# Reassociating the second product of an attention + MLP + soft-MoE kernel

## The chip, the cores and the metric

One NeuronCore of a Trainium2 chip runs the whole program. The metric is device time in microseconds. TensorE (PE) multiplies and writes to PSUM; VectorE (DVE), ScalarE (ACT) and GpSimd (POOL) work element by element; SyncE (SP) issues the DMAs. PEld in the profile is TensorE's load of a stationary operand, which overlaps its matmuls.

## The reference

```python
def reference(q, k, v, moe_w_in, moe_w_out, moe2_phi, moe2_w1, moe2_w2):
    # 4 batches x 8 heads x 576 tokens x 64; heads 0-3 look back 32 tokens,
    # heads 4-7 at tokens of the same residue mod 32
    a = attention(q, k, v)                       # softmax(mask(q k^T / 8)) v
    x = a.transpose(0, 2, 1, 3).reshape(2304, 512)
    r = np.maximum(x @ w_in, 0)                  # w_in 512 x 2048
    g = r * r
    x2 = g @ w_out                               # w_out 2048 x 512
    logits = x2 @ phi                            # phi 512 x 32
    d = softmax(logits, axis=0)                  # over the 2304 tokens
    slot_input = d.T @ x2                        # 32 x 512
    # 8 experts, 4 slots each: relu(slot_input w1[e]) w2[e], 512 -> 1024 -> 512
    c = softmax(logits, axis=1)                  # over the 32 slots
    return c @ slot_out
```

## The kernel before, in words

The 2304 tokens are cut into six blocks of T = 384. The work goes in three stretches.

The head is written out by hand in `HEAD` (L29), a list of small steps for all engines: scores (`S`), centring (`C`), exponential and normalising (`E`), transposing (`T`) and values (`V`, `U`) of the attention units. A unit is two heads of a batch; units 0 to 3 are batch 0. It also loads the weights (`l`), and converts them two tiles at a time: `split1` to `split4` (`W`, `X`, `Y`) take 64-bit words apart (ACT, then DVE) and make a high and a low float32r part (ACT, then DVE). `w_in` and `w_out` are both converted so, 32 tiles, 16 pairs; raw tiles sit in slots that converted tiles take later. Idle PE time is filled with `keep_warm` matmuls (L579).

The middle runs over g, which counts 6 blocks x 16 slices f of d_ff. PE and SP follow the program order there; the order on DVE, ACT and POOL is made by a scheduler that goes by priority, which is program order, with `square` put ahead. `gemm1(g)` (L401) has `w_in` stationary and the block's x moving, 12 matmuls of 384 columns (three high/low products of four kc); its result is h transposed, 128 of d_ff by 384 tokens. `square` and `square_low` make g's high and low part (L408 to L417). `gemm2(g-1)` (L423, L426) has g stationary and a `w_out` tile moving, 9 matmuls of 512 columns, summed over f in three banks, one for 128 tokens each. At the end of each block these sums are copied out as x2 (L439), and `Dispatch` follows, spread over the next block at `MOE_AT`: `tr` transposes x2 (L450), `logits` multiplies it by phi (L469, 32-wide weights at three column positions side by side), `soft`, `back` (L515) and `slots` (L521) hold a running maximum, running sums and a running slot input `acc`, and `comb0`, `comb1` make the softmax over slots. The attention of batches 1 to 3 runs between (`BATCHES`).

The expert weights are 64 tiles of 512 KB: `e0` to `e31` of w1, `e32` to `e63` of w2. `load_e`, `load_e_ring` and `load_e_slot` put them where room has come free: five tiles when the attention's memory goes, then the rings of x, then, all through the last block, two weight slots per g.

The tail takes the softmax of the last block to its end, makes `siT` (L773), multiplies by w1 (`gemm_a`, L812, `eh` in the trace), refills tiles (`refill`), then by w2 (`gemm_b`, L836), and forms the output from the slot outputs (`output`, L859 to L864). `gemm_b(1, 0)` is the first to need the last w2 tile; the two outputs of `slot_out`, the second half of `gemm_b` and 18 output DMAs stand behind it.

Of the kernel before, what the change touches and what calls it, by code (L numbers as in the profile page):

```python
# [28 lines left out]
HEAD = 'w0 w0 w0 w0 w0 w0 k0 q0 q2 l3 l2 q1 S0 S2 S0 w0 w0 w0 W1 l0 S2 S2 w0 S0 W1 l1 v2 w0 S0 S0 C0 w0 l4 C2 W1 E0 W1 w0 E0 W1 W1 S1 X1 X1 E2 W0 w0 Y1 E0 E2 E0 q3 w0 W0 l5 S1 E2 T0 w0 S1 T0 E2 S3 l10 w0 W0 S1 W0 T2 S1 w0 C1 W0 v0 T0 T0 l18 T0 w0 X0 T2 X0 T0 E1 T0 w0 Y1 l7 T0 S3 W0 w0 W0 E1 Y0 T2 T2 w0 v3 V0 T2 E1 E1 V0 T2 S3 w0 T2 T2 T2 l6 V0 W0 w0 C3 E3 U0 E3 T1 v1 T1 w0 l11 U0 W0 D1 W3 T1 W3 E3 w0 V2 D1 T1 E3 W2 l9 Y0 w0 D1 W3 T1 g4 V2 l15 V2 D1 U2 T3 U2 W2 V1 T3 W2 g0 W3 V1 W2 U1 g2 W3 l19 T3 T3 T3 V1 q6 g6 l20 T3 X3 Y3 T3 T3 T3 U1 g1 X3 X2 g5 V3 V3 W3 W2 Y3 U3 l16 V3 X2 Y2 l14 l8 W5 U3 S6 Y2 S6 g3 W5 W5 S6 W5 W2 R0 g7 q4 R1 g10 R1 R1 R0 W5 R0 l12 C6 E6 E6 W5 W4 g8 g14 g9 X5 l17 L1 H0 g11 E6 L0 W4 H1 W4 v6 Y5 X5 Y5 O1 W4 E6 T6 l26 W4 R2 R2 g18 R2 W7 g17 W7 T6 l13 W7 g16 g13 g12 W4 X4 Y4 O0 X4 l27 g15 l28 R3 p0 T6 g19 T6 Y4 W7 R3 R3 S4 W6 g20 l21 X7 W7 g22 S4 L3 W6 L2 H2 W7 S4 W6 R4 H3 q5 R4 R4 X7 g21 Y7 W6 S5 H4 O2 X6 W6 Y7 g23 W9 S4 L4 Y6 X6 C4 W9 E4 O3 g26 R5 E4 W9 R5 q7 Y6 W6 E4 W9 O4 E4 R5 g24 g30 W8 l22 L5 W8 T4 W9 g25 g27 H5 X9 R6 R6 l23 X9 W8 Y9 W9 T4 Y9 W11 T4 W8 g32 g28 T4 T4 g34 X8 W8 g29 R6 g35 T4 H6 W8 Y8 W11 O5 X8 W11 W10 L6 g31 R7 R7 T4 g33 R8 S7 Y8 T4 W11 O6 W10 R8 S5 W11 S5 H7 g36 R7 V6 L7 S5 R8 X11 S7 W11 W10 v4 O7 V6 X11 L8 S7 C5 g42 E5 W10 V6 E5 W10 Y11 Y11 E5 g37 O8 U6 X10 W13 l24 X10 Y10 W13 g38 g40 g39 E5 H8 Y10 V4 T5 W13 W13 U6 l25 R9 g41 W13 T5 g44 W12 g43 V4 T5 T5 C7 T5 W13 g46 U4 W10 l29 W12 R10 v5 W12 W13 g45 R9 g47 g49 g50 R10 T5 R9 R10 g48 L10 H9 H10 L9 g51 W12 W13 R11 E7 X13 T5 O10 E7 Y13 R11 l30 X12 T5 V5 R11 W12 X12 V5 O9 R12 Y12 g53 Y12 L11 g55 R12 X13 E7 U5 R12 Y13 L12 H11 g56 W14 W13 E7 T7 W14 g54 W14 W12 T7 W14 T7 g52 O11 O12 g58 T7 R13 R13 T7 T7 l31 g57 X14 R13 W14 v7 L13 X14 g59 H12 T7 Y14 T7 T7 Y14 T7 W14 W15 g62 W15 R14 R14 T7 T7 W15 H13 T7 T7 R14 T7 W15 T7 O13 L14 W15 T7 V7 X15 g60 X15 Y15 V7 H14 V7 Y15 O14 g61 U7 W15 U7 g63 R15 R15 R15 L15'.split()  # L29
BATCHES = [(1, 16, (0, 1), (4, 8), (0, 1, 2, 3, 5), (2, 1)), (2, 32, (0, 2, 1, 3), (0, 3, 6, 9), (0, 1, 2, 3, 5), (2, 1)), (3, 48, (0, 2, 1, 3), (0, 3, 6, 9), (0, 1, 2, 3, 5), (2, 1))]  # L30
MOE_AT = (1, 2, 3, 5, 7, 9, 10, 11)
ATT_END = 64
PRIO = 400
LOW = 'DDDPDDDDPPDPDPPP'
SUB = 'DDDDDDDDDDDDDDDD'
WARM = 6
# [24 lines left out]
def body(tc, qd, kd, vl, vs, win, wout, phi, w1, w2, cst, out):  # L61
# [3 lines left out]
    with ExitStack() as base, ExitStack() as order:  # L65
# [9 lines left out]
        bp = pool(base, "bp", side="right")  # L75
# [16 lines left out]
        elT = cp.tile([128, 2, 128], F32, name="elT")
# [5 lines left out]
        tf = cp.tile([128, NS], F32, name="tf")  # L98
# [3 lines left out]
        bt = bp.tile([128, 6, 512], F32, name="bt")  # L102
# [13 lines left out]
        def slot(n, shape, dt, name):  # L116
# [3 lines left out]
        bflat = bt.rearrange("p a b -> p (a b)")  # L120
# [217 lines left out]

        NW = 2 * NF
        w_in, w_out = [None] * NF, [None] * NF
        raws, ys = {}, {}

        def load_w(n):
            if n < 26:  # L350
                raws[n] = slot(n + (8 if n < 22 else 4), [128, 512, 2], U32, f"raw{n}")
            else:
# [584 lines left out]
```

## Time and profile before

| | |
|---|---|
| median of 3 runs | 558.02 us (557.0 to 558.48) |
| span of the profiled execution | 557.1 us |
| busy: PE / PEld | 535.7 us (96%) / 451.6 us (81%) |
| busy: DVE / ACT / POOL | 252.1 / 248.2 / 44.2 us |
| moved by DMA | 72.88 MB, mean 131 GB/s |
| chain that ended last, by engine | PE 80%, DMA 7%, DVE 6%, ACT 3% |
| chain, by line | L401 33%, L426 23%, L423 11% |

The profile is that of one execution, so sums are made against its span. A busy PE is not a PE at its peak, because matmuls overlap and each one's recorded duration holds its neighbours; what a matmul adds is read from the chain of waits, where pieces follow one another. A float32 matmul is recorded as two instructions, a float32r matmul and a transpose as one. "L401" is a line of the kernel before.

### The profile page before, as it was taken

What the parts mean: (1) busy time and instruction counts of PE and PEld (TensorE: products, weight loads), DVE (VectorE), ACT (ScalarE), POOL (GpSimd) and SP (SyncE); (2) the same over time, 40 slices, a digit from 0 to 9 for tenths busy, and PEclk for the clock granted to TensorE, in tenths of its full rate; (3) what the DMA queues carried; (4) which work ended last, traced back from release to release, by engine and by line L of the source; (5) the groups of instructions that cost most, each with busy time, mean ns of one, the idle gap of its engine ahead of it and who ended that gap; (6) DMA issues with size and microseconds to landing.
All of it is one profiled execution on the core that took longest, in us unless ns stands there. A gap on an engine that the chain in (4) does not pass through costs nothing.

```text
span 557.1 us, 10035 instructions
## 1 busy us (share of the span) xinstructions
PE 535.7 (96%) x4098; PEld 451.6 (81%) x4098; DVE 252.1 (45%) x593; ACT 248.2 (45%) x545; POOL 44.2 (8%) x56
## 2 busy tenths in 40 slices
PE   9689999999999999999999999999999999999993
PEld 7467888889888888888888888898899988985552
DVE  5988999841544156473265482311311113114213
ACT  1379787774442344433454343443333533334213
POOL 2101113110110010020010200000000000001000
PEclk9699999999999999999999999999999999999998
DMA  8987634210102011202011201610002557678958
GB/s 234 358 311 246 253 102 165 99 35 0 44 1 67 24 44 44 82 25 81 25 44 51 74 25 39 259 44 1 0 2 98 186 220 251 227 267 333 388 199 288
DMA packets 27118, 72.88 MB, mean 131 GB/s; under 512 B 3008, under 2 KB 8640, under 8 KB 27072
## 3 DMA queue, kind: packets, MB, share of 16 engines
q1 hardware_dynamic: 27072, 72.24, 37.2%
q8 instruction: 32, 0.52, 0.4%
q14 instruction: 14, 0.11, 0.1%
HBM read 67.51 MB, written 4.72 MB: 130 GB/s over the span
## 4 chain that ended last, share of the span: by engine, by line
PE 80%; DMA 7%; DVE 6%; ACT 3%; issue 1%; SPq 1%; POOL 1%; DVEq 0%; ACTq 0%; POOLq 0%
PE h L401 33%; PE acc_ps L426 23%; PE acc_ps L423 11%; DMA k<-kd 3%; DMA e<-w 2%; DMA ring<-w 2%; PE oa L313 2%; PE ob L313 2%; PE x2t L450 1%; DVE w L388 1%; PE lg L469 1%; PE qa L193 1%; PE acc_ps L836 1%; PE warm L579 1%; DVE y L374 1%
## 5 line engine op out<-in xcount | busy, mean ns | idle before, releaser
L401 PE MATMUL h<-xr,w 128*128 128x384 f32 x1152 | 220.5, 338 | 1.5 <-DVE xr L332 1.0
L401 PEld LDWEIGHTS h<-xr,w 128*128 128x128 f32 x1152 | 204.3, 188 | 11.2 <-DVE xr L332 1.2
L426 PE MATMUL acc_ps<-w,gh 128*128 128x512 f32 x576 | 153.1, 401 | 0.2 <-ACT gh L411 0.2
L408 ACT ACTIVATE r<-h 128x384 f32<-128x384 f32 x96 | 47.1, 490 | 196.3 <-PE h L401 194.9
L426 PEld LDWEIGHTS acc_ps<-w,gh 128*128 128x128 f32 x576 | 103.9, 188 | 24.7 <-ACT gh L411 2.9
L417 DVE TENSOR_TENSOR gl<-r,gh 128x384 fp32r<-128x384 f32 x89 | 49.9, 561 | 163.5 <-ACT r L413 159.5
L423 PE MATMUL acc_ps<-w,gl 128*128 128x512 f32 x288 | 82.2, 393 | 0.2 <-DVE gl L417 0.2
L423 PEld LDWEIGHTS acc_ps<-w,gl 128*128 128x128 f32 x288 | 53.8, 188 | 12.0 <-DVE gl L417 0.3
L411 ACT ACTIVATE gh<-r 128x384 fp32r<-128x384 f32 x96 | 50.3, 525 | 2.8
L413 ACT ACTIVATE r<-r 128x384 f32<-128x384 f32 x96 | 50.2, 525 | 2.1
L247 DVE STREAM_TRANSPOSE ptl<-sl 32x320 f32<-32x320 f32 (+2 forms) x72 | 31.3, 435 | 8.7 <-POOL sl L234 7.6
L365 ACT ACTIVATE y<-raw 128x512 f32<-128x512 f32 x26 | 17.0, 670 | 14.6 <-DMA raw<-win 13.1
L388 DVE TENSOR_TENSOR w<-y,w 128x512 fp32r<-128x512 f32 x30 | 22.2, 748 | 2.6 <-ACT w L381 2.4
L381 ACT CAST w<-y 128x512 fp32r<-128x512 f32 x30 | 18.4, 618 | 10.5 <-DVE y L374 10.4
L219 POOL TENSOR_TENSOR sl<-sl,tiny 128x640 f32<-128x640 f32 (+2 forms) x9 | 10.8, 1202 | 138.8 <-DVE tiny L216 138.8
L579 PE MATMUL warm<-el 128*128 128x256 f32 x66 | 20.3, 461 | 1.1 <-POOL el L572 1.1
L579 PEld LDWEIGHTS warm<-el 128*128 128x128 f32 x66 | 14.8, 236 | 4.1 <-POOL el L572 1.1
L374 DVE SCALAR_TENSOR_TENSOR y<-raw,y 128x512 uint32<-128x512 uint32 x26 | 17.4, 681 | 0.2
L202 DVE SCALAR_TENSOR_TENSOR sl<-qa,c 128x128 f32<-128x128 f32 (+3 forms) x18 | 6.4, 376 | 21.5 <-PE qa L193 16.5
L792 POOL MEMSET bt<- 128x512 f32 x4 | 2.0, 525 | 174.9 <-PE lg L469 172.8
L247 DVE STREAM_TRANSPOSE pts<-sw 32x512 f32<-32x512 f32 x20 | 14.1, 703 | 3.7 <-POOL sw L234 3.4
L836 PE MATMUL acc_ps<-e,bt 128*32 128x192 f32 (+1 forms) x184 | 14.9, 380 | 0.5 <-DMA e<-w 0.5
(187 smaller groups left out, 439.0 us busy)
## 6 DMA issues: line engine op xcount, KB each, us to landing
e<-w SPq DMA_DIRECT2D x49, 512.0 KB, 4.8
ring<-w SPq DMA_DIRECT2D x15, 512.0 KB, 8.2
raw<-win SPq DMA_DIRECT2D x14, 512.0 KB, 7.6
raw<-wout SPq DMA_DIRECT2D x12, 512.0 KB, 6.7
q<-qd SPq DMA_DIRECT2D x15, 288.0 KB, 3.1
k<-kd SPq DMA_DIRECT2D x30, 144.0 KB, 3.7
v<-vs SPq DMA_DIRECT2D x7, 512.0 KB, 3.2
out<-ob SPq DMA_DIRECT2D x9, 320.0 KB, 3.9
```

The lines of the kernel that those rows point to most:

```text
L247: DVE.transpose(out=dst, in_=src)
L313: PE.matmul(o[bank][64 * h:64 * h + 64, col:col + w1_ - w0], u.v[0:k, t, 64 * h:64 * h + 64], rhs, start=start, stop=stop, skip_group_chec ...
L374: DVE.scalar_tensor_tensor(out=yb, in0=raws[2 * m + z][:, :, 0], scalar=29, in1=yb, op0=ALU.logical_shift_right, op1=ALU.bitwise_or)
L388: (POOL if SUB[m] == "P" else DVE).tensor_tensor(out=w[:, 1], in0=ys[m][:, z], in1=w[:, 0].bitcast(F32), op=ALU.subtract)
L401: PE.matmul(hs[g][0][:, 0:T], w_in[f][:, a, 128 * kc:128 * kc + 128], xr[i % 3][:, x, kc, :], start=hs[g][1] == 0, stop=hs[g][1] == 11)
L408: ACT.activation(r, h[:, 0:T], AF.Relu)
L411: ACT.activation(gh[g], r, AF.Square)
L413: ACT.activation(r, r, AF.Square)
L417: (POOL if LOW[g:g + 1] == "P" else DVE).tensor_tensor(out=gl[g], in0=rs.pop(g), in1=gh[g].bitcast(F32), op=ALU.subtract)
L423: PE.matmul(a, gl[g][:, 128 * j:128 * j + 128], w[:, 0], start=False, stop=f == NF - 1)
L426: PE.matmul(a, gh[g][:, 128 * j:128 * j + 128], w[:, z], start=f == 0 and z == 0, stop=False)
L579: PE.matmul(warm[:, 0:256], a, b, start=True, stop=True)
```

## The change

The second product is never formed. Since logits = x2 phi = g (w_out phi), the kernel makes `pt` = w_out phi once (`turn_w` transposes w_out tiles, `phi_w` multiplies them by phi), and the logits from g transposed and `pt`. Since d^T x2 = (d^T g) w_out, the slot sums are taken of g, 32 x 2048 held as 128 x 512 in `acc`, and `w_out` is applied once, in the tail.

The first product is turned round: x is stationary (128 tokens) and `w_in` moves, 512 wide. There are 72 steps s (6 blocks x 4 chunks ch of 512 x 3 token groups j) with 12 matmuls each. `square` is one ReLU; `tr` transposes the four 128 x 128 parts of its result, ACT squares them on the way out of PSUM, and POOL (from block 4 on DVE) squares the untransposed copy in place. `w_in` is still converted to a high and low part, `w_out` to float32 alone. The w_out tiles' raw buffers are three (`rawp`). The head is shorter and ordered by hand for PE and SP only; what was in `HEAD` for batch 1, and the conversion of `w_out`, moves to numbered places (`PLACES`, four per step). `load_e` calls move with the buffers. The expert products and the output keep their form.

```diff
-W_ORDER = [(0, 0), (0, 1), (0, 2), (1, 0)] + [w for f in range(3, NF) for w in ((0, f), (1, f - 2))] + [(1, NF - 2), (1, NF - 1)]
+W_ORDER = [(c, kc) for c in range(4) for kc in (0, 2, 1, 3)]
+AT = [2, 8, 14, 22, 46, 60, 74, 86, 98, 110, 122, 134, 146, 158]
+OFF = [0, 4, 8, 12, 23]
+PLACES = [(0, "l16"), (0, "l17"), (0, "l18")]
+for n, p in enumerate(AT):
+    PLACES += [(AT[n - 1] + 2 if n else 0, f"q{n}"), (AT[n - 1] + OFF[4] if n else 0, f"v{n}")]
+    PLACES += [(p + o, k + str(n)) for k, o in zip("SCETV", OFF)]
+for m in range(8):
+    PLACES += [(8 + 4 * m, f"c{m + 8}")] + [(10 + 4 * m, f"l{n}") for n in range(19 + 2 * m, min(21 + 2 * m, 32))]
+PLACES += [(18 + 2 * f, f"z{f}") for f in range(16)] + [(20 + 2 * f, f"p{f}") for f in range(16)]
+TR0 = [30, 31, 32, 35, 36, 37, 40, 41, 42, 45, 46, 49]
...
+            if m < 8:
+                if m < 2:
+                    ys["t", m] = slot(16 + m, [128, 2, 512], F32, f"y{m}")
+                ys[m] = ys["t", m % 2]
+            else:
+                ys[m] = slot(8 + m, [128, 2, 512], F32, f"wo{m}")
...
+        def gemm1(s, kcs=range(4)):
...
+                for x, a in ((0, 0), (0, 1), (1, 0)):
+                    PE.matmul(hs[s][0], xr[b % 3][:, x, kc, 128 * j:128 * j + 128], w_in[ch, kc][:, a],
...
+        def tr(s):
...
+            o = ps("t", f"t{s}")
+            for y in range(4):
+                PE.matmul(o[:, 128 * y:128 * y + 128], gs[b, ch][:, j, 128 * y:128 * y + 128], ident, start=True, stop=True,
+                          is_transpose=True)
+            ACT.activation(gts[b, ch][:, :, 128 * j:128 * j + 128], o.rearrange("p (y t) -> p y t", y=4), AF.Square)
+            g = gs[b, ch][:, j]
+            (POOL if b < 4 else DVE).tensor_tensor(out=g, in0=g, in1=g, op=ALU.mult)
+        def logits(b, ch):
...
+            for y in range(4):
+                PE.matmul(lgs[b][32 * y:32 * y + 32, 0:T], pt[:, 4 * ch + y, :], g[:, y, :], start=ch == 0, stop=ch == 3,
+                          skip_group_check=True)
+        def turn_w(f):
+            o = ps("at", f"wt{f}")
...
+            ACT.copy(wts[f], o)
+        def phi_w(f):
...
+            for kc in range(4):
+                PE.matmul(pps[0][:, 32 * y:32 * y + 32], wts[f][:, 128 * kc:128 * kc + 128], ph[:, kc, :],
+                          start=kc == 0, stop=kc == 3, skip_group_check=True)
...
+            def total(self):
+                self.o = ps("mo", f"lr{self.b}")
+                PE.matmul(self.o[:, 0:T], tident, lsb, start=True, stop=True)
...
+            def turn(self):
+                o = self.o2 = ps("mo", f"lt{self.b}")
                 for j in range(3):
+                    lt = lsb[:, 128 * j:128 * j + 128]
+                    PE.matmul(o[:, 96 + 32 * j:128 + 32 * j], lt, tident[:, 0:NS], start=True, stop=True)
+                    PE.matmul(o[:, 32 * j:32 * j + 32], lt, tident[:, 0:NS], start=True, stop=False)
+                    PE.matmul(o[:, 32 * j:32 * j + 32], quarter, dg, start=False, stop=True)
+                ACT.activation(ex_, o[:, 0:96], AF.Exp)
...
+            def slots(self):
+                o = ps("mo", f"sa{self.b}")
+                for j in range(3):
+                    for ch in range(4):
+                        PE.matmul(o[32 * ch:32 * ch + 32, :], ex_[:, 32 * j:32 * j + 32], gs[self.b, ch][:, j, :],
+                                  start=j == 0, stop=j == 2, skip_group_check=True)
+                DVE.scalar_tensor_tensor(out=acc, in0=acc, scalar=al, in1=o, op0=ALU.mult, op1=ALU.add)
...
+            for kc in range(4):
+                if s > 1 or kc == 3:
+                    gemm1(s, (0, 2, 1, 3)[kc:kc + 1])
+                if kc == 3:
+                    with tc.high_priority(offset=PRIO):
+                        square(s)
+                for fn, args in bg.get(4 * s + kc, ()):
+                    fn(*args)
+            if s > 60 and s % 3 == 2:
+                for n in range(4 * ((s - 60) // 3), 4 * ((s - 60) // 3) + 4):
+                    load_e_slot(n)
...
+        o = ps("lg", "si")
+        for y in range(4):
+            for ch in range(4):
+                PE.matmul(o[32 * ch:32 * ch + 32, :], gT[:, y, 32 * ch:32 * ch + 32], w_out[4 * ch + y],
+                          start=y == 0, stop=y == 3, skip_group_check=True)
...
+        for n in range(16, 24):
+            load_e_slot(n)
```

The head in the changed order has, for PE: 24 warm matmuls, scores of units 0, 2 and 1 with warm matmuls between, values of unit 0, scores of unit 3, values of 2, the first product's kc 0 and 2 of steps 0 and 1, values of 1, kc 1, values of 3. Converts 0 and 1 stand in it; converts 2 to 7 follow it, ahead of step 0's last kc.

## Rows read from the trace of the kernel before

**Rows 1.** The page's forty slices: granted TensorE clock in tenths of full speed.

```profile
PEclk9699999999999999999999999999999999999998
```

**Rows 2.** Windows: stretch, its length, busy us (instructions) of each engine, clock, DMA.

```profile
9.80:49.05 39.25, 30.66 (x430) 24.42 (x421) 34.34 (x74) 22.01 (x54) 2.99 (x3) 0.87 0.87 297
49.05:497.40 448.35, 447.13 (x3080) 391.31 (x3081) 195.94 (x449) 207.54 (x448) 35.73 (x35) 1.00 0.27 91
497.40:557.10 59.70, 49.18 (x533) 28.74 (x532) 17.22 (x65) 17.34 (x43) 1.98 (x4) 0.95 0.82 305
```

**Rows 3.** Chain of waits, middle and start of tail: start, us, what, instructions.

```profile
371.33 2.11 PE h L401 x12
373.43 0.44 PE x2t L450 x4
373.87 1.39 PE acc_ps L426 x6
...
382.24 1.00 PE lg L469 x24
383.25 1.60 PE acc_ps L426 x6
...
400.40 0.99 PE sa L521 x6
401.39 1.59 PE acc_ps L426 x6
...
509.69 3.56 PE eh L812 x32
```

**Rows 4.** Groups by line of PE, 49.05 to 497.4: count, busy us, mean ns.

```profile
L401 PE MATMUL h<-xr,w 128*128 128x384 f32 x1133 | 216.0, 337 | 1.0 <-DVE xr L332 1.0
L426 PE MATMUL acc_ps<-w,gh 128*128 128x512 f32 x565 | 150.1, 401 | 0.2 <-ACT gh L411 0.2
L423 PE MATMUL acc_ps<-w,gl 128*128 128x512 f32 x282 | 80.1, 393 | 0.2 <-DVE gl L417 0.2
```

**Rows 5.** Timeline of PE, 10 to 20 and 505 to 513: start, us, line.

```profile
10.46 3.29 PE L579 MATMUL warm<-el 128*128 128x256 f32 x14
...
18.27 2.02 PE L579 MATMUL warm<-el 128*128 128x256 f32 x6
...
508.52 0.97 PE L773 MATMUL sit<-tf,acc 96*128 96x32 f32 x8
```

**Rows 6.** Groups by line of DVE, 9.8 to 49.05: the conversions.

```profile
L374 DVE SCALAR_TENSOR_TENSOR y<-raw,y 128x512 uint32<-128x512 uint32 x8 | 5.4, 685 | 0.0
L388 DVE TENSOR_TENSOR w<-y,w 128x512 fp32r<-128x512 f32 x7 | 4.8, 687 | 0.5 <-ACT w L381 0.5
...
L370 DVE TENSOR_SCALAR y<-y 128x1024 uint32<-128x1024 uint32 x4 | 2.8, 692 | 0.9 <-ACT y L365 0.9
```

**Rows 7.** Waits of PE, 9.8 to 49.05: us in total, times, longest.

```profile
PE qa L209 <- DMA k<-kd: 3.5, 1, 3.5
PE wide L193 <- DMA k<-kd: 2.2, 1, 2.2
```

**Rows 8.** DMA view, 497 to 537 in forty slices, then one issue group, whole span.

```profile
GB/s 365 401 406 295 287 389 385 406 426 414 406 430 406 164 12 111 377 381 303 262 381 385 377 418 422 410 426 389 422 410 410 401 422 410 406 414 328 131 29 0
DMA packets 3729, 13.61 MB, mean 340 GB/s; under 512 B 416, under 2 KB 416, under 8 KB 3725
...
raw<-wout SPq DMA_DIRECT2D x12, 512.0 KB, 6.7
```

**Rows 9.** Groups with shapes apart, whole span: one size on ACT and POOL.

```profile
L439 ACT COPY bt<-acc_ps 128x512 f32<-128x512 f32 x12 | 6.4, 590 | 4.9 <-PE acc_ps L423 4.9
...
L219 POOL TENSOR_TENSOR sl<-sl,tiny 128x512 f32<-128x512 f32 x2 | 2.1, 1044 | 35.3 <-DVE tiny L216 35.3
```

**Rows 10.** Chain of waits in the tail.

```profile
525.52 10.92 DMA e<-w
...
536.48 1.91 PE acc_ps L836 x26
```

More of the change, by code (lines that the diff above doesn't have):

```diff
@@ L415, in square_low @@
-        def square_low(g):
-            gl[g] = gp.tile([128, T], F32R, tag=f"gl{g % 2}", bufs=1, name=f"gl{g}")
-            (POOL if LOW[g:g + 1] == "P" else DVE).tensor_tensor(out=gl[g], in0=rs.pop(g), in1=gh[g].bitcast(F32), op=ALU.subtract)
-        def product(g, j, low):
-            f = g % NF
-            a, w = acc_ps[j], w_out[f]
-            if low:
-                PE.matmul(a, gl[g][:, 128 * j:128 * j + 128], w[:, 0], start=False, stop=f == NF - 1)
-            else:
-                for z in range(2):
-                    PE.matmul(a, gh[g][:, 128 * j:128 * j + 128], w[:, z], start=f == 0 and z == 0, stop=False)
@@ L530, in comb0, with sums, comb @@
+            def sums(self):
+                o = ps("t", f"su{self.b}")
+                for j in range(3):
+                    PE.matmul(o[0:32, 0:1], ex_[:, 32 * j:32 * j + 32], st[:, 15:16], start=j == 0, stop=j == 2)
+                DVE.scalar_tensor_tensor(out=s_run[0:32], in0=s_run[0:32], scalar=al[0:32], in1=o[0:32, 0:1],
+                                         op0=ALU.mult, op1=ALU.add)
+            def comb(self):
+                cv = c_all[:, 3 * self.b:3 * self.b + 3, :]
                 ACT.activation(cv, cv, AF.Exp)
[L532 to L533 removed]
@@ new lines, in body @@
+        keep_warm(WARM)
+        run(units[0].scores())
+        qk(3); vv(3)
+        for n in range(6, 16):
+            load_w(n)
+        SP.dma_start(ph, phi)
+        keep_warm(14)
+        run(units[2].scores())
+        run(units[0].center())
+        run(units[2].center())
+        keep_warm(8)
+        run(units[0].soft())
+        run(units[2].soft())
+        run(units[1].scores())
+        run(units[1].center())
+        convert(0)
+        transposed(0)
+        transposed(2)
+        run(units[1].soft())
@@ new lines, in body @@
+        order.enter_context(tc.manual_schedule())
+        tr(NSTEP - 1)
+        load_e_ring(2)
+        logits(NBLK - 1, 3)
+        d = Dispatch(NBLK - 1)
+        d.copy()
+        d.total()
+        weights_o = [ps("at", "ct00"), ps("at", "ct01")]
+        for z in range(2):
+            weights_t(0, z, weights_o[z])
+        d.turn()
+        d.slots()
+        d.sums()
+        d.comb()
+        for z in range(2):
+            weights_out(0, z, weights_o[z], make_cw)
+        weights_o = [ps("at", "ct10"), ps("at", "ct11")]
```

562 lines of the change are left out of this document (240 added, 322 removed).

## The prediction

> **What bounds the kernel now.** I read the page's forty slices first: from the third to the last but one the granted clock reads 9 tenths or more, the top level of 2.4 GHz [rows 1]. Then I cut the span in three by the windows view [rows 2]: a head up to 49.05 us, where the first product has all its inputs; a middle of 448.35 us, in which PE idles for only 1.2 us; a tail of 59.7 us after the last first-product matmul, in which DMA moves 305 GB/s. The chain of waits in the middle is PE after PE [rows 3]. So the middle is the sum of its matmuls, and that sum can be split. Twelve 384-wide matmuls add 2.11 us to the chain (0.176 each), six 512-wide ones 1.39 us (0.232 each), four transposes 0.44 us (0.11 each), the old logits 1.00 us and their successor 0.21 us more than usual (1.60 for 1.39), the old slot sums 0.99 + 0.20 us [rows 3]. The middle holds 1133 matmuls of the first product and 565 + 282 of the second [rows 4]: 1133 x 0.176 = 199.0 and 847 x 0.232 = 196.1 us. The five dispatches in it take 15 x 0.44 for transposes + 5 x (1.21 + 1.19 + 0.22) = 19.7 us (the 0.22 is the pair of transposes of `back`, two at 0.11). What is left, 448.35 - 199.0 - 196.1 - 19.7 - 1.2 = 32.3 us, is the attention of batches 1 to 3.
>
> **Part 1, the two products.** The first product changes from 1152 matmuls of 384 columns to 864 of 512: 1152 x 0.1757 = 202.4 us against 864 x 0.2317 = 200.2 us. That is nearly nothing, since both forms stream the same columns. The second product goes: 864 x 0.2317 = 200.2 us, of which 196.1 lie in the middle. ScalarE and VectorE lose the high and low parts of g; they were not on the chain.
>
> **Part 2, what takes its place on PE.** In order:
> - `tr`: 72 x 4 transposes. I take the old transposes' price, 0.43 us per four, so 71 x 0.43 = 30.5 us before the last step ends. `turn_w`: 16 x 0.43 = 6.9 us.
> - `logits`: 24 calls (23 in the middle), each four float32 matmuls of 384 columns, 32 wide, at four column positions. A float32 matmul shows as two instructions. The nearest row is the expert product `eh`: 16 such matmuls of 512 columns in 3.56 us [rows 3], four side by side, so 0.89 us per round or 1.74 ns per column. The old logits were four rounds of 128 columns, 0.89 us, and cost 1.21; the old slot sums one round, 0.89, and cost 1.19. So going into and out of the narrow form costs about 0.31 us. New logits: 384 x 1.74 ns + 0.31 = 0.98 us, x 23 = 22.5 us.
> - `slots`: three rounds, 3 x 0.89 + 0.31 = 2.98 us. `total`: 384 columns, 0.67 us. `turn`: nine float32 matmuls with a 128-wide weight and 32 columns; the nearest row is `sit`, eight instructions, four matmuls, in 0.97 us, 0.243 each [rows 5], so 2.2 us. `sums`: six instructions, at 0.042 each as in the old logits (24 in 1.00 us), + 0.31 = 0.56 us. Together 6.4 us per dispatch, 5 x 6.4 = 32 us in the middle.
> - `phi_w`: 64 matmuls of the `sit` form, 64 x 0.243 = 15.5 us. Its bounds: 64 x 2 x 0.042 = 5 us if weights load under other work, and 64 x 0.47 = 30 us by the `warm` pairs (14 instructions in 3.29 us, though of 256 columns) [rows 5]. `sit` is the same shape within a factor, so I take it.
>
> The middle's PE work is then 846 x 0.2317 = 196.0 (18 of the 864 are done in the head) + 30.5 + 6.9 + 22.5 + 32 + 15.5 + 32.3 of attention = 335.7 us, for 448.35 now.
>
> **Part 3, the head.** DVE sets it: it is busy for 34.34 of 39.25 us from 9.8 to 49.05 [rows 2], and in that time it converts four pairs of weight tiles [rows 6], each 0.69 + 2 x 0.69 + 2 x 0.69 = 3.4 us. The new head has to convert two pairs before its first product can be complete, so up to 6.9 us of DVE work come later: 49 - 6.9 = 42 us. The loads queue on SP in another order, with four more `w` tiles ahead of the inputs of pair 3 (the fourth attention unit), for which PE already waited 3.5 us on DMA [rows 7]. I take 44 us, bounds 42 to 50.
>
> **Part 4, a new wait in block 0.** `turn_w(0)` stands in PE's written order at place 18, that is at step 4, and PE passes nothing ahead of it. It reads the `w_out` tiles of convert 8. These lie in the slot that converts 0 to 6 use for their scratch tile, so convert 8 can't begin on them before convert 6 is done, and by program order convert 7 comes first too. DVE has then, counted from the start of the middle, six pairs x 3.4 = 20.6 us, 2.1 us of convert 8 (no high and low part) and some 2.5 us of the first unit of batch 1, less about 3 us which fit into DVE's idle time in the head (39.25 - 34.34 = 4.9). That is 22 to 23 us. PE meanwhile has 6 matmuls + step 2 + scores = 5 us, waits to 7 us for pairs 2 and 3, then step 3 and half of step 4: 11 us. So it stands idle for about 12 us there and 2 us at step 3. After 2.24 and 3.5 us of such idleness the old head ran at a lower clock: six warm instructions took 2.02 us (0.34 each), where fourteen took 0.235 each before it [rows 5, 7]; I add 2 us. Sum 16 us, bounds 3 (the converts fit into gaps) and 26. Queued behind it on PE are all later steps, so nothing hides it. Behind the SP queue's waits for free raw buffers (a raw tile took 6.7 us from issue to landing [rows 8]) stand the `q` and `v` loads of batch 1; with two raw tiles per 6 us of PE work I count 3 us for these and later small waits.
>
> ScalarE has two passes over 512 columns, 0.59 us each like its copies of that size, in a step of 4.4 us, GpSimd 1.04 us of squaring [rows 9]; both are covered. If GpSimd were late, `slots` would wait for it, with eight quarter steps to spare.
>
> **Part 5, the tail.** Now: 59.7 us, PE busy for 49 of them, and its end hangs on the last weight tile, after which the second expert product still runs [rows 10]: last tile at 536.4, which is 39 us after the last first-product matmul, and then 20.7 us to the end. From 497 to 537 us 13.61 MB move [rows 8], 26 tiles of 0.524 MB. The changed kernel has by the same point 3 + 5 + 6 + 12 = 26 of 64 tiles landed (raw, x1, two rings, three groups of slots), so 38 remain: `w_out` keeps eight double slots to the end, and slots come free only four at a time per three steps. 38 x 0.524 = 19.9 MB. DMA moves 406 to 430 GB/s where it is saturated, a mean of 340 with the dip in which it waited for free tiles [rows 8]. At 405: 49 us; the pause until `slots` frees the g tiles, latency and refills add 3 to 5, so the last tile lands 53.5 us after the last step, and + 20.2 makes 74 us (68 if PE's own path, 20 us of softmax, slot sums and w_out and then the present 47.5 us, binds; 80 at the 340 mean). So 14 us are given back here.
>
> The Trainium skill's "DMA: Bandwidth & Descriptors", Specifications, gives about 358 GB/s as the HBM limit of a core. The trace exceeds it for 20 us on end, so the measured rate is used; by the page's figure the 19.9 MB would take 56 us, and the sum would be some 6 us more.
>
> **Sum.** 44 + 335.7 + 16 + 3 = 399 us to the last step, + 74 = 473 us of span. The profiled span of before, 557.1, lies 0.9 us under the 558.02 median, so 474 us, 15% less.
>
> **Rivals.**
> - *No wait in block 0.* DVE keeps up and PE's own path binds the tail: 474 - 13 - 6 = 455 us. For it: DVE had 4.9 us idle in the head, and the scheduler may place convert 8 in gaps. Against: the shared slot. 10%.
> - *The w_out chain paces block 0.* Each further pair of `turn_w` waits for a raw buffer, a 6.7 us load, ScalarE and 2.1 us of DVE: 9 us a pair instead of 6, seven times, + 21: 495 us. Against: three raw buffers let load and convert overlap. 19%.
> - *The clock falls.* Block 0 holds 64 + 48 transposes and thin matmuls. If PE ran them at 1.2 GHz, its 68 us of work would take some 55 more: 529 us. Against: the old transposes run at the full granted clock, in a stream of full matmuls [rows 1, 3]; here too half of the time is full matmuls. 4%. The Trainium skill's "TensorE: Matmul & The Clock Gate", Part 4: PE-mode transpose, says that transposes do not count as PE-busy; the trace has none apart from full matmuls, so it can't refute that.
> - *The change loses.* If the four column positions ran one after another, logits (24 x 3 x 0.67), slots (6 x 9 x 0.89) and the 16 final matmuls (12 x 0.89) would add 107 us: 581 us, slower. It loses from an overlap below 1.2. Against: `eh` in the same form, and the old logits, whose 24 instructions took 1.00 us where 12 single rounds would take 2.7. 2%.
>
> **How the numbers follow.** My forecast, 474 us (462 to 486), has 60%; the four rivals 10, 19, 4 and 2; 5% are unnamed. The range takes in the first two rivals and the unknown prices (phi_w -10/+14, head -2/+6, tail -6/+6): 452 to 503. A difference under about 0.3% can't be measured here; faster by more 0.96, same 0.01, slower 0.03.
>
> **What would show it.** Right: first-product groups of 864 at 2.78 us per twelve in the chain; the new logits near 0.98 us; PE idle of some 12 us before `turn_w`'s first transpose, released by DVE's `wo` tile; the last first-product matmul near 399 us; a tail of 74 us whose chain holds DMA of expert tiles. Wrong: logits of 2.5 us and more (no overlap), PE clock of 0.5 in block 0, waits between `turn_w` calls, or idle PE in blocks 1 to 3 on attention, ScalarE or GpSimd.

## The result, and the profile after

The changed kernel takes 486.06 us (median of four runs, 482.56 to 490.36) where the kernel before takes 557.51 in the same series: 0.869 of the time, 95% interval 0.864 to 0.874. A second series on another occasion gave 486.02 us (481.43 to 489.56), ratio 0.864 (0.860 to 0.868). The ratios leave out runs over 1.5% above the fastest of the same kernel, among them the profiled runs of the first series and of e5_no_shift_or. The forecast was 474 us (462 to 486) with a range of 452 to 503 for all cases: the sign and the size are right, 12 us are missing from the sum, and the result stands at the upper edge of the narrower range.

The changed kernel's time depends on the run more than that of before does: the same code ended at 481 and at 490 us, and the part on the clock below shows where two of its traces part. The rows here are of the second series, whose profiled run took 483.24 us with a span of 481.5.

The windows view of the changed kernel, cut where [rows 2] cut the old one, with the first 51 us of the middle split off; columns as there:

```profile
9.80:48.66 38.86, 27.52 (x452) 24.08 (x452) 36.15 (x77) 22.98 (x56) 3.43 (x3) 0.88 0.98 345
48.66:62.00 13.34, 3.02 (x14) 1.91 (x7) 13.24 (x24) 10.05 (x18) 0.00 (x0) 0.50 0.06 15
62.00:100.00 38.00, 33.76 (x286) 26.62 (x287) 25.56 (x60) 16.50 (x33) 7.14 (x10) 0.94 0.55 179
100.00:403.00 303.00, 300.72 (x2337) 219.97 (x2335) 118.64 (x281) 109.05 (x208) 68.60 (x67) 1.00 0.26 86
403.00:481.50 78.50, 60.51 (x563) 29.66 (x562) 15.63 (x57) 14.93 (x35) 1.94 (x4) 0.88 0.81 309
```

PE is still busy for 300.72 of 303 us from 100 to 403, so the middle is still the sum of its matmuls. What is new is the stretch from 48.66 to 62, where PE works for 3 us and VectorE for 13.24 of 13.34, and a tail of 78.5 us instead of 59.7. The head did not shrink: 48.66 for 49.05.

The chain of waits of the changed kernel in the middle (start, us, what, instructions), which answers to [rows 3]:

```profile
297.36 1.39 PE h L407 x6
298.75 0.78 PE lg L435 x8
299.53 1.58 PE h L407 x6
301.11 0.44 PE t L424 x4
301.55 2.76 PE h L407 x12
...
311.68 0.64 PE lr L473 x2
...
317.97 0.69 PE h L407 x3
318.67 2.71 PE sa L497 x24
321.38 0.90 PE h L407 x3
322.27 0.28 PE su L504 x6
322.55 1.58 PE h L407 x6
```

Twelve 512-wide matmuls take 2.76 us, as forecast (12 x 0.2317 = 2.78), and nothing but PE stands in this chain. Six matmuls behind the logits take 1.58 us where six alone take 1.39: the 0.19 belong to the logits' price. The waits of PE from 48 to 100 us (us in total, times, longest), and ScalarE's timeline just before the longest of them ends (start, us, line, operation):

```profile
PE h L407 <- ACT g L416: 10.3, 1, 10.3
PE qa L203 <- DMA k<-kd: 2.8, 1, 2.8
PE pp L453 <- DVE pt L456: 1.1, 1, 1.1
```

```profile
57.51 1.24 ACT L371 ACTIVATE wo<-raw 128x512 f32<-128x512 f32 x2 [1.19 <-DVE w L392]
58.63 1.15 ACT L386 CAST w<-y 128x512 fp32r<-128x512 f32 x2
60.71 0.67 ACT L371 ACTIVATE wo<-raw 128x512 f32<-128x512 f32 x1 [0.93 <-DVE w L392]
61.28 1.07 ACT L416 ACTIVATE g<-h 128x512 f32<-128x512 f32 x2
```

There is a wait of 10.3 us in block 0, but it isn't the one that was forecast. Step 2's matmuls wait for a bank that the ReLU of step 0 has to read first (L416), and this ReLU stands on ScalarE behind the casts and splits of conversions 2 to 9, each of which waits in its turn for VectorE (releaser L392). The first `turn_w`, at 73.39, follows the matmul before it without a wait.

The chain in the tail, which answers to [rows 10], and the DMA view of the tail in forty slices, which answers to [rows 8]:

```profile
411.29 4.43 PE sa L497 x22
...
421.56 6.71 DMA e<-w
...
428.33 10.82 DMA e<-w
439.17 10.19 DMA ring<-w
...
449.43 10.11 DMA e<-w
...
459.58 3.35 PE so L838 x26
```

```profile
GB/s 338 317 404 421 141 0 0 313 380 402 400 415 419 419 409 407 415 400 407 411 411 417 396 411 409 411 409 183 15 8 0 223 322 130 324 354 355 357 328 0
```

Nearly 38 us of the chain are expert tiles on their way. The last lands at 459.5, which is 56.5 us after the last first-product matmul (403.03), and 22 us of work follow it.

### The profile page after: what moved, and what is told of

The parts are those of the page before. It is cut to its first block, busy times and chain, and to the rows that moved or that the text cites. A ratio compares the mean times of both kernels' runs of the same rounds, so it can differ in the third digit from the quotient of the medians.

```text
span 488.6 us, 9028 instructions
## 1 busy us (share of the span) xinstructions
PE 443.3 (91%) x3726; PEld 317.5 (65%) x3726; DVE 213.5 (44%) x502; ACT 174.5 (36%) x348; POOL 84.2 (17%) x97
## 4 chain that ended last, share of the span: by engine, by line
PE 71%; DVE 11%; DMA 9%; ACT 3%; issue 2%; POOL 1%; SPq 0%; DVEq 0%; POOLq 0%; ACTq 0%
PE h L407 39%; PE t L424 6%; DMA e<-w 6%; PE sa L497 4%; PE lg L435 3%; PE pp L453 3%; DMA ring<-w 2%; PE oa L323 2%; PE ob L323 2%; PE warm L556 2%; DVE ptl L257 2%; PE qa L203 2%; PE wt L441 2%; PE so L838 1%; DVE w L392 1%
## 5 line engine op out<-in xcount | busy, mean ns | idle before, releaser
L407 PE MATMUL h<-w,xr 128*128 128x512 f32 x864 | 239.0, 414 | 11.6 <-ACT g L416 11.6
L407 PEld LDWEIGHTS h<-w,xr 128*128 128x128 f32 x864 | 155.2, 192 | 59.2 <-issue 19.9
L428 POOL TENSOR_TENSOR g<-g 128x512 f32<-128x512 f32 x48 | 50.2, 1045 | 129.0 <-PE t L424 99.1
L426 ACT ACTIVATE gt<-t 128x512 f32<-128x512 f32 x72 | 43.1, 598 | 75.6 <-PE t L424 75.0
L416 ACT ACTIVATE g<-h 128x512 f32<-128x512 f32 x72 | 42.8, 596 | 74.8 <-PE h L407 74.7
L424 PE MATMUL t<-c,g 128*128 128x128 f32 x288 | 44.6, 277 | 0.7 <-ACT g L416 0.7
L424 PEld LDWEIGHTS t<-c,g 128*128 128x128 f32 x288 | 35.3, 143 | 9.9 <-ACT g L416 1.1
L435 PE MATMUL lg<-gt,pt 128*32 128x384 f32 x192 | 20.5, 498 | 0.7 <-ACT gt L426 0.7
L497 PE MATMUL sa<-g,ex 128*32 128x512 f32 x144 | 18.4, 648 | 1.6 <-DVE c_all L491 1.6
L556 PE MATMUL warm<-quarter 128*128 128x128 f32 x116 | 18.1, 327 | 1.0 <-POOL quarter L551 1.0
```

Of the source, the lines that this page charges most:

```text
L407: PE.matmul(hs[s][0], xr[b % 3][:, x, kc, 128 * j:128 * j + 128], w_in[ch, kc][:, a], start=hs[s][1] == 0, stop=hs[s][1] == 11)
L416: ACT.activation(gs[b, ch][:, j], h, AF.Relu)
L424: PE.matmul(o[:, 128 * y:128 * y + 128], gs[b, ch][:, j, 128 * y:128 * y + 128], ident, start=True, stop=True, is_transpose=True)
L426: ACT.activation(gts[b, ch][:, :, 128 * j:128 * j + 128], o.rearrange("p (y t) -> p y t", y=4), AF.Square)
L428: (POOL if b < 4 else DVE).tensor_tensor(out=g, in0=g, in1=g, op=ALU.mult)
L435: PE.matmul(lgs[b][32 * y:32 * y + 32, 0:T], pt[:, 4 * ch + y, :], g[:, y, :], start=ch == 0, stop=ch == 3, skip_group_check=True)
```

## The experiments

Four questions: is the wait in block 0 set by ScalarE's order, by VectorE's work, or by something behind it; do the 32-wide matmuls overlap as the prices assumed; is the tail bound by DMA; and what does the clock cost. The table gives each kernel's median, its ratio to the kernel before with the interval, the time of the run that was profiled, the end of the last first-product matmul in that trace, and the clock that TensorE was granted from 62 to 100 us. A trace is of one run, which lies up to 6 us off the median.

| kernel | us | ratio (95%) | profiled run | last product ends | clock 62 to 100 |
|---|---|---|---|---|---|
| changed, first series | 486.06 | 0.869 (0.864-0.874) | 490.36 | 408.81 | 0.81 |
| a0_changed_again | 486.02 | 0.864 (0.860-0.868) | 483.24 | 403.03 | 0.94 |
| e1_relu_first | 483.41 | 0.864 (0.861-0.868) | 480.79 | 400.80 | 0.88 |
| e2_slots_by_column | 501.22 | 0.898 (0.894-0.902) | 500.30 | 417.79 | 0.90 |
| e3_eight_tiles_less | 472.23 | 0.848 (0.843-0.854) | 472.12 | 402.82 | 0.94 |
| e4_low_part_half_on_pool | 491.92 | 0.879 (0.875-0.883) | 492.19 | 410.46 | 0.78 |
| e5_no_shift_or | 481.82 | 0.862 (0.860-0.864) | 488.01 | 406.34 | 0.72 |
| e6_tail_warm | 486.19 | 0.869 (0.864-0.875) | 486.69 | 407.59 | 0.81 |
| e7_first_and_pool_and_warm | 489.91 | 0.876 (0.872-0.881) | 490.00 | 411.60 | 0.78 |
| e8_k_loads_ahead | 484.21 | 0.865 (0.861-0.869) | 486.01 | 404.97 | 0.79 |
| e9_scores_in_other_bank | 481.51 | 0.861 (0.856-0.865) | 481.92 | 402.35 | 0.87 |
| e10_no_shift_or_k_ahead | 478.32 | 0.856 (0.853-0.859) | 477.90 | 395.55 | 0.92 |

**The change again.** No edit.

> The changed kernel as it is, on the same chip as the experiments beside it. Every theory expects 483 to 490 us, with the last first-product matmul near 400 to 409 us and a tail of 77 to 80 us.

Measured 486.02 us, with the rows above.

**The ReLUs first.** The last quarter of steps 0 and 1 and their ReLUs go ahead of conversions 2 to 7 in the program:

```
-        for m in range(2, 8):
-            convert(m)
...
+        for s in range(2):
+            gemm1(s, (3,))
+            with tc.high_priority(offset=PRIO):
+                square(s)
+        for m in range(2, 8):
+            convert(m)
...
```

> Steps 0 and 1 and their ReLUs come ahead of converts 2 to 7 in program order; nothing else moves. Theory A: PE's 11.6 us at 49 us is a place in ScalarE's order (the ReLU that frees the bank of h stands behind the copies of converts 2 to 7), so the wait goes, and PE reaches turn_w(0) near 61 us, where convert 8 is done on DVE near 63: 2 us of wait are left, the clock falls less, 7 to 12 us faster, 475 to 479 us. Theory B (the step of the prediction: turn_w(0) waits for convert 8): the wait only moves there, gain 0 to 4 us. Theory C: DVE's converts pace block 0 as a whole; the start of block 1 does not move, gain below 2 us.

Measured 483.41 us, at the same ratio as the changed kernel itself, 0.864. PE's waits in its trace from 46 to 100 us:

```profile
PE qa L203 <- DMA k<-kd: 4.6, 2, 2.6
PE qa L219 <- DVE ss L222: 4.0, 1, 4.0
PE h L407 <- ACT g L416: 2.2, 1, 2.2
```

The wait for ReLU falls from 10.3 to 2.2 us, but other waits take most of these 8 us: 4.0 stand now before the scores of batch 1's third unit, whose bank VectorE has not read (L222, at 60.84, behind its last conversion), and 2.6 before those of the second. The first `turn_w` begins at 70.35 instead of 73.39, and the last product ends 2.2 us earlier. So ScalarE's order decides where PE waits, and not how long: theory A's 7 to 12 us are not there. VectorE's run of conversions from 47 to 62 us is the next candidate.

**Half of VectorE's subtractions on GpSimd.** e1_relu_first, and in conversions 2 to 7 the subtraction of the second tile goes to GpSimd:

```
-                DVE.tensor_tensor(out=w[:, 1], in0=ys[m][:, z], in1=w[:, 0].bitcast(F32), op=ALU.subtract)
+                (POOL if m > 1 and z else DVE).tensor_tensor(out=w[:, 1], in0=ys[m][:, z], in1=w[:, 0].bitcast(F32), op=ALU.subtract)
```

> On top of the run with the ReLUs first: of converts 2 to 7 the second tile's low part is made by GpSimd, which is idle there; DVE has 6 x 0.69 = 4.1 us less to do between 48 and 63 us. Theory A (DVE's order holds PE, by whatever instruction): turn_w(0), at 70.4 us with the ReLUs first, comes 3 to 5 us earlier; 477 to 480 us. Theory B (the loads of raw tiles and of q and k on SP pace block 0): under 1.5 us.

Measured 491.92 us: 8.5 us slower than without GpSimd, or 8 by the ratios. VectorE's or-operations from 48 to 62 us in e1_relu_first (count, busy us, mean ns), then from 48 to 64 in this kernel, then GpSimd's group there, then two pieces of this kernel's timeline (start, us):

```profile
L380 DVE SCALAR_TENSOR_TENSOR y<-raw,y 128x512 uint32<-128x512 uint32 x8 | 5.2, 688 | 0.0
```

```profile
L380 DVE SCALAR_TENSOR_TENSOR y<-raw,y 128x512 uint32<-128x512 uint32 x8 | 8.4, 1092 | 0.0
```

```profile
L392 POOL TENSOR_TENSOR w<-y,w 128x512 fp32r<-128x512 f32 x5 | 7.3, 1470 | 12.1 <-ACT w L386 12.1
```

```profile
51.26 1.55 POOL L392 TENSOR_TENSOR w<-y,w 128x512 fp32r<-128x512 f32 x1 [2.66 <-ACT w L386]
51.59 1.76 DVE L380 SCALAR_TENSOR_TENSOR y<-raw,y 128x512 uint32<-128x512 uint32 x1
```

VectorE has four subtractions in place of nine, yet its eight or-operations take 8.4 us in place of 5.2, while GpSimd needs 1470 ns for what VectorE does in 686. The mean of 1092 ns is a mixture: the three or-operations that begin while GpSimd subtracts take 1.76 to 1.78 us, the other five 0.68 to 0.69. VectorE reaches the read that frees the third unit's bank (L222) at 64.76 instead of 60.84, and the first `turn_w` began at 75.74, 5.4 us later than in e1_relu_first. The helper took from VectorE more time than it gave. Of the 9.7 us by which the last product ends later in the trace, 4.2 are idle time of PE; the rest is PE at a lower granted clock (0.78 for 0.88 from 62 to 100 us).

**VectorE's shift and or left out.** e1_relu_first without them in conversions 2 to 7:

```
-            run(split2(m))
+            if not 1 < m < 8:
+                run(split2(m))
```

> On top of the run with the ReLUs first: converts 2 to 7 leave out the shift and the or of the low word on DVE, so twelve w_in tiles hold wrong values; DVE has 6 x 2.06 = 12.4 us less before convert 8. Theory A (DVE paces block 0): turn_w(0) comes 8 to 12 us earlier, at 58 to 62 us, and as much comes off the total: 470 to 475 us. Theory B (loads on SP pace it): under 4 us. Theory C (ScalarE's copies and splits, 2.5 us a pair, pace it then): 4 to 8 us.

Measured 481.82 us. Three fifths of VectorE's work on conversions 2 to 7 is gone. In the trace the first `turn_w` begins 5 us earlier (65.36), and PE is idle for 3.3 us less up to the last product [rows under "Both edits at once"]; the median shows 1.6 us. So the 12.4 us of VectorE's work that are left out are worth some 3 us of PE's idle time, not theory A's 8 to 12. SP's timeline of this kernel (start, us, line, loads) and two pieces of PE's show what PE meets next:

```profile
55.93 15.52 SPq L359 DMA_DIRECT2D raw<-wout  x4
71.54 0.38 SPq L151 DMA_DIRECT2D q<-qd  x1
71.98 0.47 SPq L152 DMA_DIRECT2D k<-kd  x1
```

```profile
53.68 0.63 PE L203 MATMUL qa<-k,q 128*32 128x128 f32 x12 [2.99 <-DMA k<-kd]
76.27 1.07 PE L203 MATMUL qa<-k,q 128*32 128x128 f32 x12 [0.39 <-DMA k<-kd]
```

SP stands for 15.5 us in front of `w_out` tiles whose buffers are not yet free, and the `q` and `k` loads of the fourth unit of batch 1 are queued behind them. PE waited for that `k` until 76.27, but in this trace for 0.39 us only; the wait of 3.0 us stands at 53.68, for the `k` of another unit, which is not queued there. (The expectation of e10_no_shift_or_k_ahead has the two mixed up.) In e1_relu_first SP stood there for 12.5 us and PE waited 2.0 us for that `k`, in the changed kernel 9.7 and 2.8. The next three runs ask whether SP's queue is a second gate behind VectorE's.

**The `k` loads ahead.** e1_relu_first, with tiles 21 and 22 of `w_out` loaded at place 16, behind the fourth unit's loads, instead of at place 14.

> e1_relu_first with one more change: the loads of w_out's raw tiles 21 and 22 stand behind the q and k loads of batch 1's fourth unit on SP, not ahead of them. In e1_relu_first SP stood 12.5 us (61.96 to 74.46) in front of raw tiles whose buffers were not free, and the k load behind them was issued at 74.98 and landed at 78.86; PE waited 2.0 us for it. If SP's order is the gate there, the load is issued near 63, PE's wait for it goes, and the last step ends 2 us earlier: 481.4 us. If VectorE's work in the head and the first steps is the gate, the next buffer is late in its place, and less than 0.7 us is gained.

Measured 484.21 us, no gain. The loads went out at 63.94 instead of 74.55 and PE no longer waited for that `k`; two of the waits that are left:

```profile
PE pp L453 <- DVE pt L456: 2.1, 1, 2.1
PE pp L453 <- ACT wt L446: 2.0, 1, 2.0
```

These two `phi_w` waits were 1.1 and 1.2 us in e1_relu_first: part of what the queue gave, the next waits took. Yet PE's idle time up to the last product is 1.6 us less than in e1_relu_first. The last product ends 4.2 us later all the same, because PE is busy for 5.8 us longer with the same matmuls, at a granted clock of 0.79 for 0.88 from 62 to 100 us. So the median doesn't decide between the theories.

**Another bank for the first unit's scores.** e8_k_loads_ahead, with the first unit of batch 1 in a bank of its own:

```
-                    un = us[n] = Unit(b, u, b0, ("at", "at") if u < 2 else ("mo",), part=part)
+                    un = us[n] = Unit(b, u, b0, ("at", "at") if u < 2 or n == 0 else ("mo",), part=part)
```

> e8_k_loads_ahead with one more change: the scores of batch 1's first unit go to one of the two banks named at, so that those of its third unit don't wait for VectorE to read the bank mo. In e1_relu_first PE waited 4.0 us there (qa L219 for DVE L222). If the bank is the gate, these 4.0 us go, less some 1 us for the k load: 3 us less than e8_k_loads_ahead. If VectorE's order is the gate (the read stands behind six conversions in either kernel), PE comes sooner to the ReLU of step 2, which is as late as before, and its 2.2 us wait there grows to 5 or 6: less than 1 us is gained.

Measured 481.51 us, 2.7 less than e8_k_loads_ahead, with intervals that overlap. By the trace the wait for L222 is gone; the wait for ReLU is 3.7 us in place of 3.2, the waits before the scores of the first two units are 3.7 together in place of 2.1, and the first `turn_w` begins 1.3 us earlier (69.34 for 70.60). PE's idle time up to the last product is the same within 0.2 us (14.2 for 14.4). The 2.6 us by which the last product ends earlier are busy time, at a clock of 0.87 for 0.79. So the waits speak for the second theory, and the median's gain is no evidence for the first.

**Both edits at once.** e5_no_shift_or with the `k` loads ahead as in e8_k_loads_ahead.

> e5_no_shift_or (which leaves out the shift and the or of conversions 2 to 7, so that the low bits of these tiles are wrong) with the q and k loads ahead of the raw tiles as in e8_k_loads_ahead. In e5_no_shift_or SP stood 15.5 us in front of raw tiles, and PE waited 3.0 us for k at 76. If two gates stand one behind the other, VectorE's work and then SP's order, the two edits together give what neither gave alone: the last step 4 to 5 us earlier than in e1_relu_first, 478 to 479 us. If the time is spent elsewhere (the clock after the waits, the chain of loads and conversions of w_out), it stays at 481 to 482.

Measured 478.32 us, as forecast, and the last product ends at 395.55, 5.3 us before that of e1_relu_first. Alone the two edits changed the median by -1.6 and +0.8 us; together by -5.1. That looks like two gates, one behind the other. The windows view from 46 us to the last product in e1_relu_first, e5_no_shift_or, e8_k_loads_ahead, e9_scores_in_other_bank and this kernel (first numbers: length, PE busy; third from the end: clock) says otherwise:

```profile
46.00:400.80 354.80, 338.77 (x2692) 249.47 (x2692) 159.87 (x368) 137.44 (x262) 75.81 (x76) 0.99 0.28 94
46.00:406.34 360.34, 347.57 (x2692) 256.70 (x2692) 151.27 (x353) 133.95 (x258) 75.12 (x76) 0.96 0.28 93
46.00:404.97 358.97, 344.58 (x2692) 253.32 (x2692) 159.52 (x368) 137.15 (x262) 75.55 (x76) 0.97 0.28 93
46.00:402.35 356.35, 342.14 (x2692) 251.76 (x2690) 158.71 (x366) 136.53 (x260) 75.64 (x76) 0.98 0.28 94
46.00:395.55 349.55, 337.87 (x2692) 248.71 (x2692) 150.90 (x353) 132.79 (x255) 75.16 (x76) 0.99 0.29 95
```

Length less busy time is PE's idle time: 16.0, 12.8, 14.4, 14.2 and 11.7 us. Alone the two edits take 3.3 and 1.6 us of it, together 4.4, so their gains nearly add: leaving out shift and or takes 3.3 us without and 2.7 with the `k` loads ahead. What the two edits alone lost again is busy time for the same 2692 matmuls, at a lower granted clock. By the ratios the two together gain 3.6 us more than the sum of each alone, and the uncertainty of that figure is as large. So VectorE's conversions and SP's queue each hold PE for a few us. That one of them hides the other is not shown, nor whether the lower clock in the profiled runs of e5_no_shift_or and e8_k_loads_ahead comes of the edits or of chance.

**The slot sums column by column.** The two loops of `slots` are exchanged, so that three matmuls in a row go to the same 32 columns of the array, not to four different ones in turn:

```
-                for j in range(3):
-                    for ch in range(4):
+                for ch in range(4):
+                    for j in range(3):
```

> The twelve matmuls of slots are issued column position by column position, three after one another at each, instead of round the four positions; the work is the same. Theory A (four positions run side by side only when neighbours in the order differ): slots takes 9 to 12 rounds of 0.89 us instead of 3, so 8 to 10.5 us instead of 2.78, + 5 to 8 us at each of six dispatches, 32 to 46 us slower in all. Rival: the overlap is not what makes it cheap (a queue reorders, or the price is per instruction): less than 5 us slower.

Measured 501.22 us, 15 more: neither theory A's 32 to 46 nor the rival's 5. The chain of this kernel at the second dispatch:

```profile
328.14 5.36 PE sa L497 x24
```

24 instructions of 512 columns take 5.36 us in this order, 0.223 us each, and 2.71 us [in the chain above] in the order of the changed kernel. So the overlap of the four positions is worth a factor of 1.98, and an instruction alone costs about what one of the first product's 512-wide matmuls costs (0.23). Theory A is right in kind; it had one matmul alone at the price of a whole round, 0.89 us, and it takes two instructions of 0.223. The Trainium skill's "TensorE: Matmul & The Clock Gate", Part 3: Packing small matmuls, has 2.38 for three column tiles; these four float32 ones gave 1.98.

**Eight expert tiles less.** The loads of expert tiles 56 to 63 are left out.

> The last 8 of the 64 expert tiles are not loaded; the second expert product reads earlier tiles in their place, so this leaves out 4.2 MB of loads and the right values of experts 4 to 7 there. Theory A: the tail hangs on the last tile at some 405 GB/s, so 8 x 1.29 = 10.4 us come off the landing, of which PE's own path lets 8 to 11 through: 475 to 478 us. Rival: the tail is PE's own path (softmax, slot sums, w_out, two expert products) at a lower clock: under 2 us faster.

Measured 472.23 us. The last product ends at 402.82 as in the changed kernel (403.03), so all the difference lies in the tail: 67.5 us for 78.5. PE's longest wait there, and the chain where the tiles stood:

```profile
PE sa L497 <- DVE c_all L491: 1.0, 1, 1.0
```

```profile
441.26 10.54 PE so L841 x192
```

With 4.2 MB less the tail is PE's own path, with no DMA anywhere in its chain from the last product to the end, and 67.5 us is what the prediction gave for that case (68).

**Warm matmuls in the tail.** Thirteen warm-up matmuls in the tail's waits, from the last ReLU to the slot sums.

> The changed kernel with 13 more 128-wide warm matmuls in the waits of PE between the last step and slots (3 us of PE time in waits of 0.7, 0.7, 0.6 and 1.0 us); nothing else. Theory A (the clock falls after these waits; slots took 4.43 us there and 2.71 in the middle): the last step to the end of slots takes 10.5 to 11.5 us instead of 12.7, DMA's pause is shorter by as much, and 1 to 2.5 us come off the tail of 78.5. Rival: the clock is not set by these waits; the warm matmuls only add up to 1 us.

Measured 486.19 us, no gain that can be measured. In its trace the slot sums run at full clock:

```profile
415.88 2.74 PE sa L497 x22
```

They took 4.43 us in the changed kernel. From the last product to the end of the slot sums 11.0 us pass instead of 12.7, as theory A has it, and the tail is 77.3 us for 78.5. That the total gains by it is not shown: this run's last product ended 4.6 us later, and the unchanged kernel's own tails differ as much (78.5 and 79.8 us in the two series).

**Three edits together.** e4_low_part_half_on_pool with the warm matmuls of e6_tail_warm.

> ReLUs first, half of the low parts on GpSimd, and the warm matmuls in the tail, together. If the three are separate: 2.6 + 4 + 2 us less than the changed kernel, 475 to 479 us. If a later stage takes the gains back: 480 to 484 us.

Measured 489.91 us, 2 us less than e4_low_part_half_on_pool: GpSimd's cost is all there, and the warm matmuls' share is within the spread.

**What the clock costs.** Up to the last product the changed kernel's two series, e3_eight_tiles_less and e6_tail_warm run the same instructions. The windows view of the first series from 62 to 100 us (the row for the second series stands above) and from 82 to 88, then of the second series from 82 to 88:

```profile
62.00:100.00 38.00, 34.10 (x257) 27.08 (x258) 24.85 (x58) 14.71 (x29) 5.90 (x8) 0.81 0.51 171
82.00:88.00 6.00, 6.00 (x24) 5.31 (x23) 2.42 (x8) 2.16 (x4) 1.22 (x2) 0.50 0.45 171
```

```profile
82.00:88.00 6.00, 6.00 (x66) 5.21 (x66) 3.84 (x9) 3.87 (x9) 1.23 (x2) 1.00 0.42 168
```

At 0.81 (the first series and e6_tail_warm) the last product ends at 408.81 and 407.59, at 0.94 (the second series and e3_eight_tiles_less) at 403.03 and 402.82. A mean clock of 0.81 between levels of 1 and one half means that 38% of 38 us, 14.4, ran at the lower level, one of 0.94 means 4.6 us; the 9.9 us between them at half speed are 4.9 us of work lost. The ends differ by 4.6 to 6.0 us, of which 1.2 to 1.8 are more idle time of PE and the rest is busy time. So between these four traces the difference is made in block 0. In all four the clock is at 0.50 in the last 4 us of the long wait, 58 to 62, and back at 1.00 from 68. They part later: behind PE's wait for `k` that ends near 81 us it falls to 0.50 again in the first series and e6_tail_warm, after 2.0 us of waiting, and stays at 1.00 in the second series and e3_eight_tiles_less, after 2.8 and 3.0 us. Why, no run here shows. The runs of the second series that took 489 us were not profiled, so whether they lost their time in the same place is open too.

## Why the prediction came out as it did

The predicted span was 472.7 us and the one shown is 481.5. The difference is 4.7 (head) + 2.0 (PE's work) - 2.3 (waits) + 4.5 (tail) = 8.9 us. The run that was profiled lies another 2.8 us under the median; no trace shows what its slower neighbours lost.

**Products (part 1): right.** 2.76 us per twelve, and the middle is shorter by the second product.

**PE's new work (part 2): the sum right, one reason wrong.** The middle lasts 403.03 - 48.66 = 354.4 us; without 14.4 us of waits before 100 us and 2.3 after it, 337.7 us are work, and the forecast was 335.7. About 7.7 us of this work ran at the lower clock level (the 3.0 us before 62 us and, by the mean of 0.94, 4.6 behind it), which is 3.8 us lost; I had 2 us for the clock and booked them under the wait. By terms: transposes 0.44 (0.43); logits 0.78 + 0.19 on the next six matmuls = 0.97 (0.98); slots 2.71 + 0.21 = 2.92 (2.98); total 0.64 (0.67); turn 1.90 + 0.09 (2.2); sums 0.28 + 0.19 = 0.47 (0.56); `phi_w` 0.81 per four matmuls, 0.20 each (0.243).
The price per column came from `eh`, a row of the same form in the same arrangement, so it held. What I made of it did not: I took the 0.89 us of a round of four for the price of one matmul alone, so that the four overlapped fourfold. One alone is two instructions of 0.223 us, 0.45, and the four overlap by 1.98 (e2_slots_by_column). Therefore the rival "the change loses" was priced on a wrong footing. Without overlap at 1.98, logits and slots would cost about 24 x 0.78 x 0.98 + 6 x 2.71 x 0.98 = 34 us more, the final product another 4, and the change would still win; 581 us was not to be had from it.

**The head (part 3): wrong.** 48.66 for 44. I counted six pairs of conversions behind the start of the middle. VectorE did part of them earlier: from 48.66 on only eight subtractions, eight or-operations and three shifts of conversions 2 to 7 remain, 5.2 + 5.2 + 2.1 = 12.5 us where I had 20.6. It was busy for 36.15 of 38.86 us in the head, more than before [rows 2], so the conversions filled the gaps between the attention's steps, and the head kept its length; this is read from the sums, and no run tests it. I had named this gap (4.9 us) and booked it only in part 4. Another 1.4 us are a wait that I had not counted there: the last inputs of the first product were written by 47.25 us, but PE's order has the scores of batch 1's first unit ahead of it, and PE waited for their `k` until 47.55.

**The wait in block 0 (part 4): the size right, the place wrong.** 14.4 us of waits up to 100 us and 2.3 after it, where I had 16 (2 of them for the clock) + 3. The step that failed is the order: I followed VectorE's work to the operand of `turn_w(0)` and forgot to follow PE through the steps ahead of it, whose bank is freed by a ReLU that shares ScalarE with the same conversions. Since both stand behind VectorE's conversions, the size came out nearly the same; that is in part luck, since leaving out three fifths of VectorE's work took only 3.3 us of PE's idle time (e5_no_shift_or). VectorE was done with the `w_out` tiles of conversion 8 at 62.6 us where I had 66 to 67: what the head is longer, the run of conversions behind it is shorter, and the two errors partly cancel. The later waits behind SP's queue, which I set at 3 us, are there (2.8 us for `k`), and e8_k_loads_ahead and e10_no_shift_or_k_ahead show that this wait goes when the loads stand ahead in the queue.

**The tail (part 5): the mechanism right, the size 4.5 us short.** It is bound by DMA (e3_eight_tiles_less: 11 us less with 4.2 MB less, which at 405 GB/s are 10.4). The last tile lands 56.5 us after the last product instead of 53.5. Part of that is the pause in the DMA view, two slices at 0 GB/s: SP waits there until the slot sums have read the g tiles (10.7 us on PE `sa`), and the slot sums took 4.43 us at the lower clock instead of 2.71. Behind the last tile come 22 us instead of 20.2 (the chain of before, [rows 10], has 20.6). In [rows 8] the rate exceeds 358 GB/s for 16 us on end, not 20; here it does so for 38 us.

**The rivals.** "No wait" is out. "The w_out chain paces block 0" is out at its price of 21 us: between two `turn_w` PE waits at most 1.1 us, plus 2.8 for `k`. "The clock falls" holds in a small way: not because transposes run by themselves (the stretch from 62 to 100 us is full of them and has a mean of 0.94 in the run shown), but behind PE's waits, for 3 to 5 us of busy time between traces of the same instructions. That rival took the sentence of the Trainium skill's "TensorE: Matmul & The Clock Gate", Part 4: PE-mode transpose, on transposes that don't count as busy, to put all of block 0 at the lower level; with full matmuls between the transposes, no run here shows that. "PE clock of 0.5 in block 0", which I had named as a sign of being wrong, did come, from 46 to 66 us in the trace shown, mostly while PE stood idle.

## What to carry to other kernels

When a change moves work into a stretch where another engine is full, follow that engine's queue to every buffer it frees, not only to the operand that you have in mind; the first instruction in the waiting engine's order that needs any of them is where the wait stands. Judge an edit worth a few us by PE's idle and busy time in the traces too, and not by the median alone: here the granted clock cost as much as the edits gave, differently from run to run, and the medians looked like gates that hid one another where the idle times nearly added. Take prices from rows of the same form and the same arrangement, and test the arrangement before you build a rival on it.

## What had not been expected of the hardware

- Four float32 matmuls at the four column positions overlap by a factor of 1.98, not 4 (5.36 us for 2.71).
- An or-operation of VectorE (128x512, uint32) that began beside a GpSimd subtraction took 1.76 to 1.78 us instead of 0.69. GpSimd's subtractions there took 1470 ns on average, where its multiplication of the same size takes 1050 in the changed kernel; none of them ran alone.
- In the DMA-bound tail the core moved 396 to 419 GB/s for 18 slices on end (36 us), as long as no load waited for a free tile.
- Waits of 2 to 10 us in block 0 can cost twice: the wait, and work at half clock behind it, worth 3 to 5 us between traces of the same instructions. The same wait for `k` was followed by half clock in two traces and by full clock in two others.
